# Spacing the first bursts, moving one conv burst, dropping one filler and moving the last store in a fused conv and SwiGLU kernel

## The chip, the cores and the metric

The kernel runs on one core of a Trainium2 chip. The metric is the device time of one execution in microseconds; a time here is a median of several executions unless it says "mean".

## The reference, cut to what matters

```
# x: 8 x 4096 x 192, weight: 8 heads x 7 taps
w = softmax(weight, axis=-1)                     # over the 7 taps
out[b, s, head] = sum_k w[head, k] * x_pad[b, s + k, head]    # causal conv of 7 taps
y = (silu(out @ w_gate) * (out @ w_val)) @ w_out              # d_model 192, d_ff 1536
```

The kernel gives float32, and works in fp16 with float32 accumulation.

## The kernel before

Tokens go in 64 blocks of 512. A block has 12 steps (`NCH = 12`, n counts them through all blocks). One step is six matmuls of 512 columns, which run as three pairs on the two row halves of the array (a "gate pair" below; in before's trace a gate and a val matmul both start at 40.63 us, 64 rows each), then ScalarE's silu and VectorE's product give one tile h. After every third step a burst of "down" matmuls multiplies finished h tiles with w_out. The conv is done by matmuls too. Blocks 0 to 3 have "early" convs; the later blocks come in units of four (a unit is 48 steps), whose conv goes to a scratch tensor in DRAM and comes back transposed (`fetch`). For unit 1 two conv bursts run during steps of unit 0.

```
# one conv burst of a unit: matmuls, then copies out of the banks by ScalarE and VectorE
at = (28, 31) if u == 0 else (10, 22)      # steps of unit u with unit u+1's two conv bursts
...
gate_val(n)
...
elif n in (9, 11):
    slot(1 if n == 9 else 2, b, silu[n - 1], work)     # work: early conv of block 2 at step 11
elif n == 13:
    slot(3, 0, silu[n - 1])
elif j % 3 == 1 and b:                                 # from step 13 on: every third step
    k = {1: 3, 4: 4, 7: 1, 10: 2}[j]
    slot(k, b - 1 if j < 7 else b, silu[n - 2], work if j > 4 else None)
    if j == 4 and work:
        work()                                         # step 28: conv after the burst
...
if u + 1 < NU:
    if ls == at[0]:
        conv_dup(u + 1)                    # GpSimd: copy 64 columns of the conv's result
    if ls == at[1]:
        for m in range(2): conv_out(u + 1, m)          # SyncE: store to scratch
    if ls == at[1] + 1:
        for m in range(2, 8): conv_out(u + 1, m)
    lo = 32 if u == 0 else 28
    if ls in range(lo, lo + 12, 3):
        fetch(UB * (u + 1) + (ls - lo) // 3)           # SyncE: transposing loads
if u + 2 < NU:
    if ls == (22 if u == 0 else 1):
        x16_tile(u + 2)
        load_x(u + 2, 0, silu[n - 1])      # GpSimd issues the loads of x
    if ls == (25 if u == 0 else 5):
        load_x(u + 2, 1, silu[n - 1])
    if ls == (29 if u == 0 else 26):
        dup_x(u + 2)                       # SyncE: duplicates x, waits for both loads
```

The argument `silu[n - 1]` of a burst is a wait: the two row halves swap their accumulator banks from burst to burst, and the kernel has a burst begin only after the one ahead of it has finished; the silu of a step in between stands for that. At the start, filler matmuls keep TensorE busy until the taps are ready:

```
keep_warm(7)            # 7 matmuls of 512 columns
spread_taps()
keep_warm(5, P)         # 5 of 128
make_wide()
early(0, ...)           # conv of block 0
eturn(0, ...)           # its transposes
```

## Time and profile before

| | before |
|---|---|
| time, first three executions | 792.62 us (792.59 to 793.4) |
| span of the profiled execution | 790.9 us |
| PE busy | 783.5 us, 99% |
| first gate pair starts | 9.01 us |
| lost to silu waits at steps 9, 11, 13 | 0.61 us |
| first conv burst of unit 1, what it costs PE | 1.28 us |

The page of the kernel before, its first part (busy time and share of the span), the clock row of its second part and the chain of waits:

```profile
PE 783.5 (99%) x12007; PEld 526.7 (67%) x12007; DVE 582.9 (74%) x928; ACT 522.1 (66%) x910; POOL 67.6 (9%) x95
...
PEclk9999999999999999999999999999999999999999
...
PE 97%; POOL 1%; DMA 1%; DVE 0%; ACT 0%; issue 0%; POOLq 0%
```

TensorE (PE) bounds the kernel. In the steady part a gate pair starts every 0.215 us and 12 down matmuls take 0.50 us, without a gap. The timeline of weight loads (PEld) of the first bursts, with start, duration, count and, in brackets, the idle time before and what ended it:

```profile
18.32 0.94 PEld L564 LDWEIGHTS <-h 64*128 64x128 f16 x24 [0.51 <-ACT sig L547]
20.82 0.94 PEld L564 LDWEIGHTS <-h 64*128 64x128 f16 x24 [0.51 <-ACT sig L547]
24.58 0.94 PEld L564 LDWEIGHTS <-h 64*128 64x128 f16 x24 [0.51 <-ACT sig L547]
```

These are the waits for a silu at steps 9, 11 and 13. PE itself loses 0.19 to 0.21 us at each: its pairs ended at 18.13, 20.61 and 24.37. The PE timeline around the first conv burst (`cv`), cut to what matters:

```profile
41.27 0.66 PE L564 MATMUL acc<-wo,h 64*128 64x192 f16 x12
41.86 0.73 PE L461 MATMUL cv<-x,band 64*32 64x240 f16 x32
42.52 0.40 PE L538 MATMUL gate<-xc,w 64*128 64x512 f16 x1
...
43.87 0.37 PE L538 MATMUL val<-xc,w 64*128 64x512 f16 x1 [0.19 <-DVE tm L478]
...
44.99 0.83 PE L564 MATMUL acc<-wo,h 64*128 64x192 f16 x12
```

From 41.27 to 44.99 us PE does 12 down matmuls (0.50) and nine gate pairs (1.94) besides the conv, so the conv costs 3.72 - 2.44 = 1.28 us: the gate pairs behind it need the banks that it filled (the val matmul at 43.87 waits 0.19 us for VectorE's copy out of them).

### The profile page before, as it was taken

What the parts mean: (1) busy time and instruction counts of PE and PEld (TensorE: products, weight loads), DVE (VectorE), ACT (ScalarE), POOL (GpSimd) and SP (SyncE); (2) the same over time, 40 slices, a digit from 0 to 9 for tenths busy, and PEclk for the clock granted to TensorE, in tenths of its full rate; (3) what the DMA queues carried; (4) which work ended last, traced back from release to release, by engine and by line L of the source; (5) the groups of instructions that cost most, each with busy time, mean ns of one, the idle gap of its engine ahead of it and who ended that gap; (6) DMA issues with size and microseconds to landing.
All of it is one profiled execution on the core that took longest, in us unless ns stands there. A gap on an engine that the chain in (4) does not pass through costs nothing.

```text
span 790.9 us, 28567 instructions
## 1 busy us (share of the span) xinstructions
PE 783.5 (99%) x12007; PEld 526.7 (67%) x12007; DVE 582.9 (74%) x928; ACT 522.1 (66%) x910; POOL 67.6 (9%) x95
## 2 busy tenths in 40 slices
PE   8999999999999999999999999999999999999997
PEld 5666666666666666666666666666666666666665
DVE  7677777777777777768777777777777777777775
ACT  6666666666666666766667666666667667676664
POOL 8101010010100101001010000100001010000000
PEclk9999999999999999999999999999999999999999
DMA  9999565787747778467894857857477784726211
GB/s 139 151 199 152 125 116 115 157 121 151 125 104 143 131 145 135 104 133 118 158 138 113 121 112 164 126 143 130 94 149 127 150 120 111 134 80 121 75 42 42
DMA packets 213825, 99.22 MB, mean 125 GB/s; under 512 B 147256, under 2 KB 212800, under 8 KB 212800
## 3 DMA queue, kind: packets, MB, share of 16 engines
q1 hardware_dynamic: 167424, 78.75, 47.4%
q0 software_dynamic: 46000, 18.45, 20.6%
q8 instruction: 94, 1.54, 0.8%
q14 instruction: 35, 0.29, 0.1%
q10 hardware_dynamic: 272, 0.20, 0.1%
HBM read 36.89 MB, written 41.16 MB: 99 GB/s over the span
## 4 chain that ended last, share of the span: by engine, by line
PE 97%; POOL 1%; DMA 1%; DVE 0%; ACT 0%; issue 0%; POOLq 0%
PE gate L538 61%; PE acc L564 32%; PE cv L461 2%; PE val L538 1%; DMA xe<-in_x_dram 1%; POOL w L167 0%; POOL xe L97 0%; PE acc L585 0%; PE cv L372 0%; PE turn L430 0%; DVE h L549 0%; ACT sig L547 0%; DVE tm L478 0%; ACT o_sb L718 0%; DVE o_sb L620 0%
## 5 line engine op out<-in xcount | busy, mean ns | idle before, releaser
L549 DVE TENSOR_TENSOR h<-sig,val 128x512 f16<-128x512 f16 x768 | 507.6, 688 | 195.8 <-PE val L538 194.3
L547 ACT ACTIVATE sig<-gate 128x512 f16<-128x512 f32 x768 | 458.6, 597 | 235.1 <-PE val L538 208.8
L538 PE MATMUL val<-xc,w 64*128 64x512 f16 x2304 | 539.2, 376 | 0.2 <-DVE tm L478 0.2
L538 PE MATMUL gate<-xc,w 64*128 64x512 f16 x2304 | 539.3, 376 | 0.0
L538 PEld LDWEIGHTS <-w 64*128 64x128 f16 x4608 | 254.0, 110 | 183.9 <-issue 1.6
L564 PEld LDWEIGHTS <-h 64*128 64x128 f16 x6096 | 257.4, 94 | 62.8 <-issue 6.1
L564 PE MATMUL acc<-wo,h 64*128 64x192 f16 x6096 | 298.8, 243 | 0.1
L97 POOL DMA_DIRECT2D x<-in_x_dram x40 | 31.5, 792 | 436.3 <-ACT sig L547 427.6
L478 ACT CAST tm<-cv 128x480 f16<-128x480 f32 x60 | 30.6, 562 | 22.0 <-PE cv L461 22.0
L478 DVE CAST tm<-cv 128x480 f16<-128x480 f32 x60 | 36.7, 653 | 2.6
L620 DVE COPY o_sb<-acc 128x384 f32<-128x384 f32 x63 | 34.7, 550 | 0.0
L489 POOL COPY tm<-tm 128x1280 f16<-128x1280 f16 x15 | 18.8, 1254 | 137.0 <-DVE tm L478 116.0
L619 ACT COPY o_sb<-acc 128x384 f32<-128x384 f32 x63 | 30.2, 480 | 0.0
L461 PE MATMUL cv<-x,band 64*32 64x240 f16 x960 | 18.2, 265 | 0.0
L461 PEld LDWEIGHTS <-band 64*32 64x32 f16 x960 | 10.1, 91 | 4.9 <-issue 4.7
L132 POOL MEMSET x<- 6x192 f16 x7 | 1.7, 248 | 59.7 <-PE cv L461 59.6
L97 POOL DMA_DIRECT2D xe<-in_x_dram x9 | 5.9, 672 | 0.8 <-DMA xe<-in_x_dram 0.6
L636 PE MATMUL warm<-fill 128*128 128x512 f16 (+1 forms) x12 | 3.9, 496 | 1.2 <-DVE fill L91 1.2
L390 ACT CAST tme<-cv 128x288 f16<-128x288 f32 x8 | 2.9, 401 | 2.6 <-PE cv L372 2.6
L372 PEld LDWEIGHTS <-wide 64*64 64x64 f16 x256 | 2.7, 108 | 2.0 <-ACT wide L330 1.0
L372 PE MATMUL cv<-xe,wide 64*64 64x72 f16 (+1 forms) x256 | 3.2, 192 | 0.7 <-ACT wide L330 0.6
L430 PE MATMUL turn<-ident,tme 128*128 128x128 f16 x45 | 3.1, 220 | 0.5 <-ACT tme L390 0.5
(52 smaller groups left out, 37.7 us busy)
## 6 DMA issues: line engine op xcount, KB each, us to landing
out_dram<-o_sb SPq DMA_DIRECT2D x63, 384.0 KB
scr<-tm SPq DMA_DIRECT2D x105, 130.0 KB
x<-x SPq DMA_DIRECT2D x28, 480.0 KB
x<-in_x_dram POOLq DMA_DIRECT2D x24, 480.0 KB, 9.0
x<-in_x_dram POOLq DMA_DIRECT2D x7, 468.0 KB, 7.1
xc<-scr SPq DMA_TRANSPOSE x180
scr<-tm SPq DMA_DIRECT2D x15, 104.0 KB
w<-in_moe_w_gate_dram POOLq DMA_DIRECT2D x3, 192.0 KB, 5.3
```

The source lines that it names most:

```text
L97: nc.gpsimd.dma_start(out=t[p0 + i0 : p0 + i1, w0 - at : w1 - at, :], in_=bass.AP(tensor=x_flat.tensor, offset=(t0 + size * w0 - pad + i0) ...
L372: nc.tensor.matmul(o[Q * c : Q * c + Q, at : at + w], wide[Q * r : Q * r + Q, a, h, :], xe[e][Q * r : Q * r + Q, c : 2 * G : 2, h * grp : ...
L461: nc.tensor.matmul(banks[r][32 * c : 32 * c + 32, t * w : t * w + w], band[Q * r : Q * r + Q, h, :], x16[u][Q * r : Q * r + Q, NG * c : NG ...
L478: eng(tm[u][:, NG * r : NG * r + NG, 2 * grp * hp : 2 * grp * hp + 2 * grp].rearrange("p g (t e) -> p g t e", t=2), banks[r][:, 0 : 2 * w] ...
L489: seq(nc.gpsimd.tensor_copy(tm[u][:, :, SL * Q : 4 * Q], tm[u][:, :, 0:Q]))
L538: nc.tensor.matmul(o, w16[m][p0 : p0 + Q, k, e::E], xc[b][k][p0 : p0 + Q, 0:TB], start=(k == 0), stop=(k == SL - 1),)
L547: silu[n] = seq(nc.scalar.activation(sg, g, AF.Silu)).ins
L549: seq(nc.vector.tensor_tensor(hj, sg, v, op=ALU.mult))
L564: nc.tensor.matmul(acc[b][bank][:, s, :], hj[p0 : p0 + Q, ts(2 * bank + s, P)], wo16[p0 : p0 + Q, j, :], start=(not second and j == 0 and ...
L619: seq(nc.scalar.copy(o_sb[:, 0:2, :], acc[b][0]))
L620: seq(nc.vector.tensor_copy(o_sb[:, 2:4, :], acc[b][1]))
L636: nc.tensor.matmul(warm[:, 0:width], fill[:, 0:P], fill[:, 0:width], start=True, stop=True, skip_group_check=True,)
```

## The change

The intent: take these waits out, start a little earlier, end a little earlier. The diff, cut to what matters:

```
 slot(), k == 3:
-            down(b, [(True, G[2]), (False, G[3])], 1, after)
+            down(b, [(True, G[2])], 1, after)
+            if between is not None:
+                between()
+            down(b, [(False, G[3])], 1, None)

-    keep_warm(7)
+    keep_warm(6)
     spread_taps()
-    keep_warm(5, P)
+    keep_warm(3, 2 * P)

-        if n in (11, 19):            # early conv of block 2 (and 3)
+        if n in (12, 19):
-        at = (28, 31) if u == 0 else (10, 22)
+        at = (25, 31) if u == 0 else (10, 22)

-        elif n in (9, 11):
-            slot(1 if n == 9 else 2, b, silu[n - 1], work)
-        elif n == 13:
-            slot(3, 0, silu[n - 1])
-        elif j % 3 == 1 and b:
+        elif n in (9, 12, 15, 17):
+            k = {9: 1, 12: 2, 15: 3, 17: 4}[n]
+            slot(k, 0, silu[n - 1 if k == 4 else n - 2], work)
+        elif j % 3 == 1 and n > 18:
             k = {1: 3, 4: 4, 7: 1, 10: 2}[j]
-            slot(k, b - 1 if j < 7 else b, silu[n - 2], work if j > 4 else None)
-            if j == 4 and work:
-                work()
+            slot(k, b - 1 if j < 7 else b, silu[n - 2], work)

-    seq(nc.scalar.dma_start(out=o_rows[:, 2:4, :], in_=o_sb[:, 2:4, :]))
+    seq(nc.sync.dma_start(out=o_rows[:, 2:4, :], in_=o_sb[:, 2:4, :]))
```

More of the change, by code (lines that the diff above doesn't have):

```diff
@@ L656, with work @@
         work = None
-        if n in (11, 19):
-            def work(e=2 if n == 11 else 3):
+        if n in (12, 19):
+            def work(e=2 if n == 12 else 3):
                 early(e, (gate_bank, gate_bank, val_bank))
-        at = (28, 31) if u == 0 else (10, 22)
+        at = (25, 31) if u == 0 else (10, 22)
         if u + 1 < NU and ls in at:
```

## The prediction

> **What bounds it.** TensorE. The page has PE busy 783.5 of 790.9 us (99%) at full granted clock; the chain of waits is 97% PE. From 47 us on nothing stops it: the timeline has a gate/value pair every 0.215 us, 24 down matmuls in 0.99, 12 in 0.50. The change can touch the first 9 us, steps 9 to 31 (18 to 47 us) and the tail.
>
> **Fillers.** Before, seven 512-column fillers run from 1.20 us, 0.43 us apart; the taps' matmul starts at 4.30 though its input was ready at 3.75 (timeline). One less starts it 0.43 us sooner, and the first gate pair moves from 9.01 to about 8.6. But the chain runs elsewhere: GpSimd's DMA issue, the load of xe[1] (7.74 to 13.75), the early conv of block 1 at 13.79, for which PE already waits 0.3 us. That load waits for nothing of PE, so the earlier start only lengthens the wait: gain 0, at most 0.4. [...]
>
> **Bursts of block 0.** Those at steps 9, 11 and 13 wait for the silu of the step just before (weight loads idle 0.51 us "<-ACT sig"): PE starts at 18.32, 20.82, 24.58 where pairs ended at 18.13, 20.61, 24.37: 0.61 us lost. At 9, 12, 15 with the silu two steps back: -0.6. Paid back: the burst at 17 (was 16) now waits for silu 16: +0.2. It is a step nearer to block 2's transposes (step 18), which need the accumulator banks emptied: ScalarE's copy (0.48) and VectorE's (0.55, behind two products of 0.67) end later than PE gets there: +0.35. Partly returned: the burst at 19 no longer loses its 0.27 us (12 matmuls took 0.77). Net about -0.3 us.
>
> **First conv burst of unit 1**, from step 28 (after a down burst, gate/value behind it) to 25 (inside one). Now the next gate/value matmuls wait for its evacuation: from 41.27 to 44.99 us PE does 12 downs and nine pairs, 2.44 us of work, plus the conv: 1.28 us for it. The chain shows silu, product, o_sb and tm copies there, and PE waits 0.2 us "<-DVE tm". Inside a burst later (132.77 to 134.89, 36 downs) a conv costs 0.63. So -0.65, perhaps -0.15 more at step 31, whose burst runs 0.26 us late now. Its input lands in time.
>
> **Last store on SyncE.** ScalarE's issue follows its copy at once (0.41 us); SyncE's issues take 0.37. Same bytes: 0 +-0.1.
>
> **Sum.** -0.3 -0.7, and 0 to -0.2 for the ends: about 1.0 us, 0.13%: 792.6 -> 791.6 us, 80% range 790.9 to 792.5. Within 2%: 0.98; faster 0.01, slower 0.01.
>
> **What would show it.** Timeline: first gate pair near 8.6 us, but early conv of block 1 still at about 13.8; no idle "PEld acc <-ACT sig" at steps 9, 12, 15, one at 17; a gap inside the transposes at step 18; conv inside the burst at step 25 and no PE wait on tm. Everything after 47 us only shifted.
>
> **What would make it wrong.** xe[1] landing earlier outside the profile (up to 0.4 us more gain); [...] a bigger bank wait at step 18; the conv at 25 delaying evacuations.

Cut from the recorded text, where marked, is what it said of when TensorE's matmuls turn to their full rate: a rule that no trace of this case shows, the expectation drawn from it that they would turn no later, and the risk that they would.

## The result, and the profile after

The kernel after took 792.91 us (791.91 to 793.54, six runs), the kernel before 792.69 us (792.59 to 793.47, six runs) in its rounds. The ratio is 1.0000 with a 95% interval of 0.9987 to 1.0013. I had predicted 791.6 us, 1.0 us less; the time did not move.

The profiled execution of after spans 791.7 us, 0.8 us more than before's. Both traces have the same program points, so the difference can be followed along the PE timeline:

| program point | before | after | after minus before | gained (-) or lost (+) since the row above |
|---|---|---|---|---|
| first gate pair of step 6 (behind block 1's early conv) | 14.44 | 14.93 | +0.49 | +0.49 |
| end of the burst of step 19 | 32.97 | 33.15 | +0.18 | -0.31 |
| end of the burst of step 31 | 46.79 | 46.40 | -0.39 | -0.57 |
| first gate pair of step 47 | 61.95 | 61.56 | -0.39 | 0 |
| end of step 49's gate pairs | 63.89 | 64.99 | +1.10 | +1.49 |
| end of ScalarE's last copy | 786.74 | 787.87 | +1.13 | +0.03 |
| end of the span | 790.9 | 791.7 | +0.8 | -0.33 |

So the aimed-at gains are there (-0.31, -0.57, -0.33), and two losses eat them: 0.49 us at the start, and 1.49 us at step 48, far from anything that was edited. The profiled execution is one of the slower ones of after (793.53 us of 791.91 to 793.54). The loss at step 48 is in all four profiles of kernels with this order of the queues (1.16 to 1.49 us: after, and experiments 4, 12 and 13); that at the start is not: in experiment 2, with the same code up to there, step 6 begins at 13.67 us. The weight loads of after's bursts at steps 9 and 17 (timeline): only the one at 17 waits for a silu.

```profile
18.40 1.14 PEld L564 LDWEIGHTS <-h 64*128 64x128 f16 x24
...
28.23 0.44 PEld L564 LDWEIGHTS <-h 64*128 64x128 f16 x12 [0.51 <-ACT sig L547]
```

The first conv burst after, inside a burst of step 25, with no wait around it (PE timeline, gate pairs left out):

```profile
38.52 0.66 PE L564 MATMUL acc<-wo,h 64*128 64x192 f16 x12
39.11 0.73 PE L461 MATMUL cv<-x,band 64*32 64x240 f16 x32
39.76 0.67 PE L564 MATMUL acc<-wo,h 64*128 64x192 f16 x12
```

At step 48 the kernel before has no gap (PE timeline, gate matmuls):

```profile
62.60 0.38 PE L538 MATMUL gate<-xc,w 64*128 64x512 f16 x1
62.81 0.38 PE L538 MATMUL gate<-xc,w 64*128 64x512 f16 x1
63.03 0.38 PE L538 MATMUL gate<-xc,w 64*128 64x512 f16 x1
```

And the new wait, the same of after (step 47's pairs end with the one at 61.99):

```profile
61.99 0.38 PE L538 MATMUL gate<-xc,w 64*128 64x512 f16 x1
62.21 0.38 PE L538 MATMUL gate<-xc,w 64*128 64x512 f16 x1
63.40 0.37 PE L538 MATMUL gate<-xc,w 64*128 64x512 f16 x1 [0.81 <-DMA xc<-scr]
64.13 0.37 PE L538 MATMUL gate<-xc,w 64*128 64x512 f16 x1 [0.32 <-DMA xc<-scr]
```

Step 48 is the first step of unit 1. Its three input tiles `xc` come from the scratch tensor by transposing loads, and the second and third land too late. The chain of waits of after now passes through SyncE's queue and these loads for the first time (`SPq 1%`; before it had no SPq). Why they are late is in the queues. GpSimd's timeline, before:

```profile
38.78 0.86 POOL L97 DMA_DIRECT2D x<-in_x_dram  x1 [2.01 <-ACT sig L547]
44.54 1.25 POOL L489 COPY tm<-tm 128x1280 f16<-128x1280 f16 x1 [4.90 <-DVE tm L478]
```

and after:

```profile
41.32 1.25 POOL L489 COPY tm<-tm 128x1280 f16<-128x1280 f16 x1 [4.38 <-DVE tm L478]
42.51 0.86 POOL L97 DMA_DIRECT2D x<-in_x_dram  x1
```

With `conv_dup` (the copy tm<-tm) at step 25, it stands ahead of the load of x for unit 2 in GpSimd's queue, waits 4.38 us there for the conv's result, and the load is issued at 42.51 in place of 38.78 us. SyncE's timeline (its DMA issues), before:

```profile
43.91 2.69 SPq L147 DMA_DIRECT2D x<-x  x2
47.31 6.85 SPq L497 DMA_DIRECT2D scr<-tm  x8
54.70 6.55 SPq L519 DMA_TRANSPOSE xc<-scr  x5
```

and after:

```profile
44.85 4.76 SPq L147 DMA_DIRECT2D x<-x  x2
49.70 7.48 SPq L497 DMA_DIRECT2D scr<-tm  x8
57.96 2.65 SPq L519 DMA_TRANSPOSE xc<-scr  x2
```

The duplicate x<-x waits for that load, and the conv stores scr<-tm and the transposes stand behind it. SyncE's own waits from 36 to 60 us (total, times, longest), before and then after:

```profile
SPq L147 <- DMA x<-in_x_dram: 1.5, 1, 1.5
```

```profile
SPq L147 <- DMA x<-in_x_dram: 3.2, 1, 3.2
```

The stores begin 2.39 us later although the conv bursts ended 0.39 us earlier, and the transposes 3.26 us later; the last tile for step 48 lands at 64.09 us. The other 0.87 us are lost between the first store and the first transpose, where the profile puts 1.1 us of SyncE's waiting down to a product of VectorE; no run tests that part. The trace puts the 3.2 us wait down to SyncE, and the first store is issued at 49.70 us, 0.09 us after the duplicate's two issues end (44.85 + 4.76). That this wait is the cause is so far an argument; the experiments test it.

### The profile page after: what moved, and what is told of

The parts are those of the page before. It is cut to its first block, busy times and chain, and to the rows that moved or that the text cites. A ratio compares the mean times of both kernels' runs of the same rounds, so it can differ in the third digit from the quotient of the medians. Undisturbed runs are those within 1.5% of the kernel's fastest.

```text
span 791.7 us, 28559 instructions
## 1 busy us (share of the span) xinstructions
PE 783.8 (99%) x12004; PEld 528.1 (67%) x12004; DVE 583.0 (74%) x928; ACT 522.2 (66%) x910; POOL 67.5 (9%) x95
## 4 chain that ended last, share of the span: by engine, by line
PE 98%; SPq 1%; DMA 0%; DVE 0%; ACT 0%; issue 0%
PE gate L538 61%; PE acc L564 32%; PE cv L461 2%; PE val L538 1%; PE warm L639 0%; PE turn L430 0%; DMA xc<-scr 0%; PE cv L372 0%; SPq L519 0%; PE acc L585 0%; SPq L497 0%; DVE h L549 0%; SPq L505 0%; ACT wide L330 0%; ACT sig L547 0%
## 5 line engine op out<-in xcount | busy, mean ns | idle before, releaser
L430 PEld LDWEIGHTS <-tme 128*128 128x128 f16 x45 | 3.2, 112 | 1.7 <-issue 1.1
```

The source lines that it names most:

```text
L430: nc.tensor.transpose(bank[:, g, :], tme[b][:, g, Q * k : Q * k + P], ident)
```

## The experiments

All kernels gave correct results. Where a kernel is called "after with ...", the edit is on the kernel after; "before with ..." on the kernel before.

**1. After, with the GpSimd copy back at step 28.**

```
-            if ls == at[0]:
+            if ls == (28 if u == 0 else at[0]):
                 conv_dup(u + 1)
```

> The kernel after, with only GpSimd's copy conv_dup of unit 1 put back to step 28, so that the load of the second half of unit 2 stands before it in GpSimd's queue again. Theory Q (queues in order: late copy, late load, late duplicate on SyncE, late conv stores behind it, late transposes): the load is issued near 39 us (42.5 after), the conv stores start near 47 us (49.7 after), PE's 1.5 us wait at step 48 is gone, and the time falls by 1.1 to 1.5 us against the kernel after, to about 791.6. Rival R (the wait comes of DMA traffic at that hour, or of the earlier conv itself): the wait stays and the time stays at 792.9.

Measured: 791.85 us (791.29 to 793.14), before 793.25 in the same rounds, ratio 0.9985 (0.9973 to 0.9997). The load is issued at 40.28 us, in an execution that runs 1.3 us later than after's (step 47 begins at 62.88): 22.6 us ahead of step 47, against 23.2 before and 19.1 after. SyncE waits 1.0 us for it in place of 3.2, and PE does not wait at step 48: the three steps from 47 take 1.95 us. The transposes start at 57.22 us, 5.66 us ahead of step 47; before it was 7.25, after 3.60. The stores start 13.6 us ahead of step 47 (49.24 to 62.88), in place of 11.9 after and 14.6 before. So the order of the queues decides whether PE waits, as theory Q says. Rival R falls in so far as it said that the wait would stay; but of the 3.65 us of lead that the transposes lost, 1.6 are still lost here with the load back in its place, so the earlier conv has a part, which experiment 7 shows by itself.

**2. After, with the duplicate behind the conv stores.**

```
-            if ls == (29 if u == 0 else 26):
+            if ls == (33 if u == 0 else 26):
                 dup_x(u + 2)
```

> The kernel after, with the duplicate of unit 2's x on SyncE issued at step 33, behind the conv stores, in place of 29; the load on GpSimd stays late as after. Theory Q: conv stores start near 47 us, no wait at step 48 or a shorter one, about 791.6 to 792.2. If only the late load mattered (not its place before the stores in SyncE's queue), the wait of about 1.5 us stays: 792.9.

Measured: 791.45 us (790.45 to 792.21), same rounds, ratio 0.9979 (0.9966 to 0.9992). SyncE's timeline of this kernel:

```profile
45.52 5.20 SPq L497 DMA_DIRECT2D scr<-tm  x8
50.77 0.95 SPq L505 DMA_DIRECT2D scr<-tm  x1
51.76 3.74 SPq L519 DMA_TRANSPOSE xc<-scr  x3
55.62 1.25 SPq L147 DMA_DIRECT2D x<-x  x2
```

The load is as late as after (issued at 41.26 us, behind the copy), and still nothing waits at step 48: the transposes start 8.5 us ahead of step 47 (at 60.30), in place of 3.6. It is the place of the duplicate in SyncE's queue that makes the late load matter. Whether it does so by its wait alone, or also because its transfer runs beside the stores, this run does not part.

**3. Before, with the load made late.** The same cost put into the kernel that did not have it.

```
-            if ls == (25 if u == 0 else 5):
-                load_x(u + 2, 1, silu[n - 1])
+            if ls == (27 if u == 0 else 5):
+                load_x(u + 2, 1, silu[n if u == 0 else n - 1])
```

> The kernel before, with the load of the second half of unit 2 made as late as it is after (step 27, behind the silu of step 27: issue near 42.3 us, before 38.8), and nothing else. Theory Q: conv stores start near 49.5 us and PE waits 1.0 to 1.5 us at step 48; time up 0.8 to 1.5 us on before, 793.5 to 794.2. Rival R: no change, 792.7.

Measured: 793.55 us (792.69 to 795.72), before 793.25, ratio 1.0010 (0.9996 to 1.0025). In the trace the load is issued at 40.89 us, 20.2 us ahead of step 47 (23.2 before), SyncE waits 3.8 us for it, the stores start at 48.21 us and a wait that the kernel before does not have appears in PE's timeline at step 48:

```profile
62.98 0.37 PE L538 MATMUL gate<-xc,w 64*128 64x512 f16 x1 [0.62 <-DMA xc<-scr]
```

The three steps from 47 on take 2.72 us in place of 1.94: 0.78 us lost. The sign and the place are as theory Q says, the size is below the 1.0 to 1.5 us that I wrote: the load is 1.1 us less late than after's (20.2 us ahead of step 47, after 19.1), and the conv burst is still at step 28. The time alone would not settle it: its interval contains 1.

**4. After, with before's fillers.**

```
-    keep_warm(6)
+    keep_warm(7)
     spread_taps()
-    keep_warm(3, 2 * P)
+    keep_warm(5, P)
```

> The kernel after, with before's fillers (seven of 512 columns, then five of 128). Theory C (the fillers decide when PE's matmuls turn fast): first conv of block 0 and its transposes again take about 1.3 and 1.0 us (1.7 and 1.7 after), and the time falls by 0.3 to 0.8 us. Rival P (the moment of turning fast falls differently from run to run whatever the fillers, since both kernels' times fall in two clusters 0.8 us apart): same two clusters, mean unchanged within 0.3 us. In either the wait at step 48 stays.

Measured: 793.40 us (792.25 to 795.66), ratio 1.0006 (0.9992 to 1.0020). Early conv and transposes of block 0 took 1.33 and 1.00 us here and the first gate pair is at 8.59 us, but PE then waits 0.7 us for the load of xe[1], so step 6 begins at 14.68 us, little earlier than after's 14.93. The wait at step 48 stayed (3.12 us for three steps, 1.18 lost). The start of this profile is as theory C says, but the time shows no gain; experiment 6 takes the fillers up again.

**5. Before, with the last store on SyncE.**

```
-    seq(nc.scalar.dma_start(out=o_rows[:, 2:4, :], in_=o_sb[:, 2:4, :]))
+    seq(nc.sync.dma_start(out=o_rows[:, 2:4, :], in_=o_sb[:, 2:4, :]))
```

> The kernel before with only the last store moved from ScalarE's to SyncE's queue. Theory T (the store lands sooner there: from the end of ScalarE's last copy to the end of the span 4.16 us before, 3.83 us after): about 3.8 us here, 0.3 us off the time. Rival (my prediction: same bytes, same landing; the 0.33 us is scatter between executions): 4.1 to 4.2 us, time unchanged within 0.1.

Measured: 792.30 us (791.77 to 793.03), before 793.18, ratio 0.9988 (0.9975 to 1.0001). From the end of ScalarE's last copy (786.37) to the end of the span (790.0) it is 3.63 us. Over ten traces (before, after and experiments 1 to 8), the five with the store on ScalarE have 4.07 to 4.16 us, the five with it on SyncE 3.60 to 3.83; five later traces with it on SyncE (experiments 10, 11, 13, 14 and 15) have 3.60 to 3.83 too. (The span is read to 0.1 us.) In this stretch theory T holds and my rival falls; the time's interval just contains 1. SyncE's waits of the kernel before, and of this one, for the last stores at the end:

```profile
SPq L745 <- DMA out_dram<-o_sb: 2.1, 2, 1.1
```

```profile
SPq L745 <- DMA out_dram<-o_sb: 1.1, 2, 0.6
```

The issue itself is no faster (0.41 us in both); the end of the program waits less for the stores.

**6. Before, with the new fillers.**

```
-    keep_warm(7)
+    keep_warm(6)
     spread_taps()
-    keep_warm(5, P)
+    keep_warm(3, 2 * P)
```

> The kernel before with only the new fillers (six of 512 columns, then three of 256). The taps' matmul starts near 3.9 us in place of 4.2 to 4.3. Theory P (PE turns fast at a moment that varies between executions): first gate pair either near 8.5 us (fast by the taps) or near 9.6 us (slow until then); if early, PE waits for the load of xe[1] or gains up to 0.4. Theory C (the new fillers always turn PE fast late): near 9.6 us, time 0.5 us worse. My prediction's term: gain 0, since the load of xe[1] ends last.

Measured: 793.00 us (792.28 to 794.55), ratio 0.9998 (0.9984 to 1.0012). The first gate pair is at 8.29 us and from 8.88 us on the pairs run at full rate; so the new fillers do not always mean a late start, and theory C falls. Step 6 begins at 13.70 us, 0.74 sooner than before, because xe[1] was there sooner: PE waits for it until 13.04 us here, until 13.79 in the kernel before. The time shows no gain.

**7. Before, with the conv burst at step 25 (GpSimd's copy left at 28).** The edits are `at = (25, 31)`, the split of slot 3, `work` passed to it, and the line of experiment 1.

> The kernel before with only the first conv burst of unit 1 at step 25 inside the down burst (GpSimd's copy stays at step 28, so the load is not delayed). From the end of the gate pairs of step 25 to the end of the down burst at step 31 PE is 0.6 to 0.8 us shorter than before; no wait at step 48; time 0.6 to 0.8 us under before. If the conv move itself delayed something else, the gain is not in the span.

Measured: 793.04 us (792.22 to 793.46), ratio 0.9994 (0.9981 to 1.0007). From the start of the burst of step 25 to the end of that of step 31: 7.89 us, before 8.45, after 7.88. The move is worth 0.56 us. But step 48 waited a little here too: 2.40 us for three steps, 0.46 lost. The transposes began at 56.70 us, 5.46 us ahead of step 47. Side by side, the traces show the margin: with 5.66 us (experiment 1) and more nothing is lost, with 5.46 us 0.46, with 5.24 (experiment 3) 0.78, with 3.60 (after) 1.49. So about 5.7 us is needed, and the kernel before had 1.6 us to spare. These two figures are estimates from single profiles, and 5.46 us with 0.46 lost beside 5.66 us with nothing lost shows their scatter. I had expected 0.6 to 0.8 us in the stretch and in the time, and no wait at step 48; the last two did not come. The gain of the move is real in its stretch, but the move itself takes 1.8 us of that margin (7.25 to 5.46) even with the load in its old place. Part of it can be read from SyncE's queue: the store out_dram<-o_sb of step 28's burst, which stands there ahead of the duplicate, is issued 17.29 us ahead of step 47 (at 44.87), before 18.62 us (at 43.33), since the conv that ran between that burst and step 47 now runs ahead of both. SyncE waited 1.8 us for the load here (1.5 before); the rest I did not trace.

**8. Before, with the bursts of block 0 at 9, 12, 15, 17.** The edits are those of the diff for steps 9 to 18.

> The kernel before with only the bursts of block 0 at steps 9, 12, 15, 17 and early conv of block 2 at step 12. Predicted: no wait for a silu at 9, 12, 15, one of 0.2 us at 17, about 0.3 us within the transposes of step 18, step 19's burst without its 0.27 us: from the first gate pair after block 1's transposes (step 8) to the end of the down burst of step 19, 0.2 to 0.4 us shorter than before's 16.17 us; no wait at step 48; time 0.2 to 0.4 us under before.

Measured: 792.84 us (792.07 to 796.09), ratio 1.0001 (0.9983 to 1.0018). From the first gate pair of step 8 to the end of the burst of step 19: 15.88 us, before 16.17, after 15.86. As predicted, the wait moves to step 17, the transposes at step 18 stretch from 0.95 to 1.23 us, and the burst of step 19 runs 12 matmuls in 0.59 in place of 0.77. The time does not show the 0.29 us, because of this kernel's start, told next.

**The start.** In experiment 8, with the old fillers, PE was slow until 13.4 us, and step 6 began at 16.62 us, against 14.44 in the kernel before with the same code up to there. The spacing of the gate pairs tells it. The kernel before (PE timeline, gate matmuls):

```profile
9.45 0.37 PE L538 MATMUL gate<-xc,w 64*128 64x512 f16 x1
9.66 0.37 PE L538 MATMUL gate<-xc,w 64*128 64x512 f16 x1
```

The kernel after:

```profile
9.66 0.61 PE L538 MATMUL gate<-xc,w 64*128 64x512 f16 x1
10.07 0.54 PE L538 MATMUL gate<-xc,w 64*128 64x512 f16 x1
10.45 0.38 PE L538 MATMUL gate<-xc,w 64*128 64x512 f16 x1
10.67 0.38 PE L538 MATMUL gate<-xc,w 64*128 64x512 f16 x1
```

0.41 and 0.38 us from start to start until 10.4 us, then 0.22. In seven profiles with the old fillers and without the additions below, the first gate pair lies between 8.48 and 10.06 us; in six with the new ones between 8.29 and 9.66. The moment of the full rate differs between executions, of one kernel too (after: 10.4 us here, 13.4 in experiment 12). What sets it the traces do not show: from PE's last idle stretch to the full rate it is 2.5 us in after (7.95 to 10.45), 5.1 in experiment 1 (7.92 to 13.02) and 5.5 in experiment 12 (7.92 to 13.44). The profile's granted clock does not show this state. In the kernel after it reads 1.00 for 9 to 10 us (busy time of PE, PEld, DVE, ACT and POOL, then the clock, DMA share and GB/s), where 512 columns took 0.41 us, twice the later 0.215:

```profile
9.00:10.00 1.00, 1.00 (x9) 0.71 (x9) 0.36 (x2) 0.59 (x1) 1.00 (x3) 1.00 1.21 153
```

The start scatters for a second reason, the landing of xe[1]: in experiment 3 PE finds it there at 12.95 us, in experiment 7 it waits for it until 14.56. The next two kernels test whether the idle stretches have a part in the late full rate.

**9. Before, with fillers in PE's two idle stretches** (0.56 us ahead of block 0's early conv, 0.50 ahead of its transposes).

```
+    gap = apool.tile([P, TB], fp32, tag="acc1", name="gap")
+    keep_warm(2, 2 * P, gap)
     early(0, ...)
+    keep_warm(2, 2 * P, gap)
     eturn(0, ...)
```

> The kernel before with two 256-column filler matmuls (0.43 us while slow) in each of the two idle stretches of PE ahead of the first gate pair: after the taps' matmuls, and after block 0's early conv. Theory G (the idle stretches of 0.5 us each let PE's matmuls stay slow past 9 us in some executions: 512 columns took 0.43 us until 13.0 in two profiles, 0.215 from 9.5 in others): the first gate pairs run 0.215 us apart from the start, and the five times spread less and lack the values above 794.5; mean 0.3 to 1 us under before. Rival: [...] spread and mean as before (792.5 to 795.3).

Measured: 792.33 us (791.96 to 793.12), before 792.53 (792.16 to 795.26), ratio 0.9998 (0.9985 to 1.0010). The pairs are at full rate from 9.44 us, no run is above 793.12. But the spread of five runs and one profile is thin proof, and the interval contains 1: on the time inconclusive.

**10. After, with the duplicate at step 33 and these fillers.**

> The kernel after, with the duplicate at step 33 (as a_xdup33) and the same fillers in the two idle stretches. If G and Q both hold, no wait at step 48, first gate pairs at full rate near 8.5 us, all runs near 790.5 to 791.5, mean at least 1.7 us under before. If G fails, as a_xdup33: 790.5 to 792.2.

Measured: 790.83 us (790.63 to 793.50), before 792.53, ratio 0.9979 (0.9965 to 0.9992). Four of five runs are at or below 791.36. The fifth, 793.50, was the profiled one: PE stood still for 1.60 us at 76.5 us in a down burst, and no instruction of the profile is named for it ("issue"). I have no explanation for this one stop. The first gate pair is at 8.58 us and nothing waits at step 48, but PE then waits 0.56 us for xe[1], so step 6 begins at 14.89 us, no sooner than in after. Experiment 2 had the same ratio, 0.9979, without these fillers: that they gain time is not shown.

**11. After, with both repairs of the queues** (experiments 1 and 2).

> The kernel after with both repairs of the queues: GpSimd's copy back at step 28 and the duplicate at step 33. Theory Q: conv stores start near 46 us, no wait at step 48, time as a_xdup33 within its scatter (791.5); the earlier load has nothing left to give. If the late load costs something beyond SyncE's queue, it is faster than a_xdup33 by 0.3 us or more.

Measured: 791.23 us (790.72 to 793.22), ratio 0.9987 (0.9974 to 1.0000), no wait at step 48. Nothing over experiment 2; it came on another chip with other scatter, so a difference of 0.3 us could not be seen either way.

**12. After once more, unchanged.**

> The kernel after, unchanged, for one more profile and times in the rounds of the others. Expected: a wait of 1.0 to 1.6 us for the transposed xc at step 48 whatever the start looks like; conv stores start 2 us or more after the end of the second conv burst; time within 0.3 us of before's mean.

Measured: 793.18 us (792.72 to 794.59), before 792.53, ratio 1.0011 (0.9998 to 1.0023). The stores start at 51.15 us, PE waits 1.0 us for the transposed tiles, pairs are slow until 13.4 us. The wait is a property of the kernel, not of one profile. The time is 0.65 us over before's by the medians, where I had expected at most 0.3.

**13. After, with the fillers in the idle stretches and nothing else.**

> The kernel after with the fillers in PE's two idle stretches and nothing else. Theory G: first gate pairs 0.215 us apart from about 8.6 us on; the wait at step 48 remains (1.0 to 1.6 us). Time 792.0 to 792.5, under the kernel after (792.9 to 793.2) by the share that the slow start has in it. Rival: start and time as after.

Measured: 792.50 us (791.63 to 793.55), before 793.26, ratio 0.9991 (0.9978 to 1.0003). Full rate from 9.02 us; the wait at step 48 is there (3.31 us for three steps, 1.37 lost). The kernel after was not timed in these rounds and the interval contains 1, so the time does not tell theory G from its rival.

**14. Experiment 2 with before's fillers.**

> a_xdup33 with before's fillers. If the fillers make no difference to the time [...]: 791.2 to 791.8, as a_xdup33, x_both. If one filler less is worth its 0.43 us: 0.3 to 0.5 us slower than those. [...]

Measured: 791.80 us (790.53 to 794.02), before 793.26, ratio 0.9983 (0.9968 to 0.9998). One filler more or less makes no difference that the scatter lets through: experiments 2 and 11, on other chips, had ratios of 0.9979 and 0.9987.

**15. Experiment 10 repeated.**

> x_gap once more. Expected 790.6 to 791.4 in all runs but for stray ones, 1.6 to 2.0 us (0.2%) under before's mean; first gate pairs at full rate near 8.6 us, no wait at step 48.

Measured: 791.67 us (791.24 to 791.86), before 793.26 (792.12 to 795.06), ratio 0.9978 (0.9965 to 0.9991). All six runs lie within 0.62 us, though most above the 791.4 that I had set as their upper end. PE's pairs at the start (PE timeline, gate matmuls):

```profile
9.31 0.37 PE L538 MATMUL gate<-xc,w 64*128 64x512 f16 x1
9.53 0.37 PE L538 MATMUL gate<-xc,w 64*128 64x512 f16 x1
```

This version beats the kernel before by 0.2% in two sets of rounds, and the kernel after in the one set that had both (experiments 10 and 12: 790.83 and 793.18 us). Experiment 2 beat the kernel before by as much without the fillers. PE still waits 0.7 us for the load of xe[1] in it, which is what is left at the start.

## Why the prediction was wrong, point by point

- **What bounds it: right.** PE is busy 99% in both kernels.
- **Bursts of block 0: right, in its parts and in sum.** Predicted -0.3 us, measured -0.31 (after) and -0.29 (experiment 8), with the wait at step 17, the stretched transposes (+0.28, predicted +0.35) and the shorter burst at 19 (-0.18, predicted -0.27).
- **Conv burst at step 25: mechanism right, size a little off.** Predicted -0.65 and perhaps -0.15 more; measured -0.57 in all. I took 0.63 us for a conv inside a burst from a later step. At steps 25 and 31 of after it costs 0.75 us each (0.59 + 0.65 + 0.51 less 1.00 for 24 downs, and 0.59 + 0.66 + 0.50 less 1.00).
- **Last store: wrong in size.** Predicted 0 ± 0.1, measured -0.33 in after and 0.5 us in experiment 5 (4.16 to 3.63).
- **"Everything after 47 us only shifted": the step that failed.** The sum had no term for unit 1's transposed input. The edit of `at` moved GpSimd's copy ahead of a load in one queue, the load's duplicate held up SyncE's queue, and of what stands behind it the conv stores began 2.39 us and the transposes 3.26 us later. That cost 1.49 us at step 48, in a stretch that I had counted as untouched. Experiments 1, 2 and 11 take the wait away at two places of the chain, experiment 3 puts one of 0.78 us into the kernel before. The late load is not the whole of it: of the 3.65 us of lead on step 47 that the transposes lost (7.25 to 3.60), 1.6 us (experiment 1) to 1.8 us (experiment 7) went with the earlier conv alone, which used up the margin; the late load took the rest.
- **Fillers: no gain in the time, as predicted, but in after's profile not for the reason given.** PE did not wait for xe[1] there at block 1's early conv; it got there at 14.26 us because its matmuls were slow until 10.4. In the profiles of experiments 4 and 6 it did wait, as I had said, 0.7 and 0.3 us. I had expected the full rate no later and named a later one as a risk; it came later. It is not shown that the new fillers bring it: it occurred in three of six profiles with them and in one of seven with the old ones, which is too few to tell, and with either the first gate pair has the same mean start (9.0 us). That share stays open. In these 13 profiles, with idle stretches of about 0.50 and 0.56 us, nine were at full rate by 9.5 us and four only at 10.4 to 13.4 us; with the stretches filled it was none of four. At a rate of four in 13 none of four would come by chance about one time in four, so that the stretches are the cause is a guess and not shown.

Without the wait at step 48 the change is worth about what its parts promise: experiment 2 is 0.2% under before (0.08 to 0.34%), against 0.13% predicted.

## What to carry to other kernels

When an edit changes the step at which work is recorded, look at every engine's queue for what is now ahead of what, not only at the engine that the edit is for: here a copy that waited 4.38 us on GpSimd's queue delayed the load recorded behind it, the duplicate that waited 3.2 us for that load on SyncE's queue delayed the stores behind it, and 20 us after the load the matmuls waited. Read from the trace, too, how much lead a transfer has before its data are needed (7.25 us here, of which about 1.6 us could be lost), since work that is moved forward can use it up by itself. Put issues that wait for far-away data behind those whose data are ready soon (experiment 2 did: no wait at step 48, ratio 0.9979). And when the scatter of the start (step 6 began between 13.61 and 16.62 us in kernels whose code up to there differs in fillers only) is larger than the gain aimed at, compare stretches of two traces between the same program points before trusting a time.
